# A backward pass of two attention branches: other pieces for the serial chain, another split of the sweep, narrower query blocks, shared transpose tiles

## The chip, the cores and the metric

The kernel runs on one NeuronCore of a Trainium2 chip. A core has five engines with their own instruction queues: TensorE (PE in the profile; PEld is its loading of weights), VectorE (DVE), ScalarE (ACT), GpSimd (POOL) and SyncE (SP), which only issues DMAs here. Each queue runs in order. The metric is the device time of one execution in microseconds, the median of several runs; lower is better.

## The reference

The reference computes an output and the gradients of eleven inputs by jax.vjp. Branch A is attention with 32 query heads of width 18 and one shared key and value head, over 2048 tokens. Branch B is a memory transformer: 64 segments of 32 tokens follow each other, each with 8 memory rows that the segment before has made, 32 heads of width 128. A sigmoid gate mixes the two.

```python
def _B_ref(x, mem0, Wq, Wk, Wv, Wo, seg_len):
    ...
    for s in range(n_seg):
        xs = x[:, s * seg_len:(s + 1) * seg_len, :].copy()
        h = jnp.concatenate([mem, xs], axis=1)
        ...
        o = jnp.einsum('bhte,hed->btd', o, Wo)
        mem = o[:, :M, :].copy()
        outs.append(o[:, M:, :])
    ...
x = A_x
g = _sigmoid((x * gate_w).sum(-1, keepdims=True))
a = _A_ref(x, A_wq, A_wk, A_wv, A_wo)
b = _B_ref(x, B_mem0, B_Wq, B_Wk, B_Wv, B_Wo, B_seg_len)
return g * a + (1 - g) * b
```

What matters: the gradient of branch B runs through the 64 segments backwards, one after the other, as each one's memory gradient is made of the next one's. Branch A has no such order.

## The kernel before

The stages follow each other on all engines: loads and projections (0 to 431 us), the forward chain of branch B woven with pass 1 of branch A (to 2130), `b_bulk` (to 2800), the backward chain of branch B woven with pass 2 of branch A (to 4325), `b_post` (to 4577), `b_dw` (to 5475) and `a_final`. The boundaries are read from the trace.

**Weaving.** TensorE works in order, and a chain would leave it idle while other engines work between its matmuls. So the chain is a Python generator that yields between pieces, and `weave` issues one sweep step of branch A at each yield (`extra` gives more or fewer steps behind single pieces, `lead` some before the first). What is issued is a fixed list per engine; nothing is decided at run time.

**A sweep step** (`a_pass2`) handles 128 queries of a head pair and 512 keys; there are 4 key blocks x 256 = 1024 steps. Two matmuls make the scores b_S (two PSUM banks, one buffer), two make b_dP (single banks, three buffers), ScalarE takes the exponential of b_S into b_E, VectorE multiplies b_dP by b_E in two halves into b_dS, and one step later four matmuls add b_E and b_dS, weighted with the transposed queries and output gradients, into the accumulator b_acc, which stays in one bank over a key block of 256 steps. The queries come from `qs_dram` as tiles b_QS: 512 columns of queries and output gradients, then 512 columns of their transposes, in which each head has 18 columns padded to 32. `a_post`, in pass 1, writes the second half. Before, one load of 256 KB serves four steps, with three buffers. 768 steps (key blocks 0 to 2) go with the backward chain, 256 with `b_dw`.

**The backward chain** (`b_chain_bwd`) has 12 pieces per segment. In order: two projections of the memory gradient with WoT (tiles r_pj and r_x, 20 matmuls each); transposes by matmul (`mem_T`) and the first `mem_grad`; the score gradient pd; 48 units of `heads`, four matmuls each into r_pj, dealt out as 4, 8, 4, 5, 9, 9, 9 with the other two `mem_grad` among them; and the last piece, which makes the next memory gradient dm from hs. r_pj and r_x have one buffer each. Among these sits `kv_mm`, work for later: it forms a 4-head block of token gradients dk or dv for the top 11 token tiles (KVT), 176 blocks, four per segment for the first 12 segments that have them (KV4), then three; `kv_out` moves it out by ScalarE and stores it. The loads of a segment, the DMA transposes of r_dT (`load_dT`, only for the lower 55 segments) and the b_QS loads all go through SP's queue in program order. `extra` adds 8 steps behind three pieces of the first segment, while the weights WT are loaded, and takes one step away in each of segments 4 to 39 (counted in the order in which they run).

**b_bulk** runs 128 groups of four heads through a software pipeline; a tick of the loop runs each stage once, on a group that many ticks back, in the order of the list `order`. The transposes go through PSUM tile x_tr with two buffers: q, k, o, v and dO (four 128x128 blocks each) and, in tiles of their own, one block of P (st_T) and of dS (st_DT). VectorE or ScalarE copies each out and so frees the buffer.

**b_post** takes the token tiles 5 to 0, forms dk and dv (`st_KV`), transposes them (`st_T`) and multiplies with WT (`st_H`). Tile 5 is one of the top 11, whose dk and dv the chain has stored already; `st_KV` forms them again and does not store them.

**b_dw** forms the weight gradients, long runs of matmuls into w_acc, with six sweep steps ahead of them and then one step whenever another WCOLS columns have streamed. Its b_QS loads go through ScalarE's queue.

Matmuls of all parts carry line 84 in the profile, transposes line 89, as helpers issue them; so they are told apart by their tiles.

Of the kernel before, what the change touches and what calls it, by code (L numbers as in the profile page):

```python
# [10 lines left out]
ALU = mybir.AluOpType  # L11
AX = mybir.AxisListType
BF16 = mybir.dt.bfloat16
# [3 lines left out]
P = 128  # L17
# [20 lines left out]
KV4 = 12  # L38
WCOLS = 4800
# [9 lines left out]
class Kern:  # L49
# [606 lines left out]
    def b_bulk(self, wp, lp, sp, psum):  # L656
# [105 lines left out]
        st_QT = lambda t: trans(t, "q", 2)  # L762
        st_KT = lambda t: trans(t, "k", 2)
# [69 lines left out]
        def st_T(t):  # L833
            tt, g, r, d = view(t)
            sc["PT", t] = transp(d["P"], r, "x_PT")

# [39 lines left out]
        def st_DT(t):  # L876
            tt, g, r, d = view(t)
            sc["DT", t] = transp(d["dS"], r, "x_DT")

# [12 lines left out]
        def st_K(t):  # L892
# [12 lines left out]
            if t % 4 == 3:  # L905
                c2 = t // 4 % 2
                for i in range(4):
# [4 lines left out]
        order = [(0, st_QT), (7, B_(0)), (0, st_KT), (7, B_(1)), (5, st_OT), (7, B_(2)), (5, st_VT), (7, B_(3)),  # L912
                 (0, st_GT), (4, st_Om), (9, st_Qm), (3, st_T), (None, st_SDm), (8, st_DT), (2, st_R), (7, st_K),
# [69 lines left out]
    def b_chain_bwd(self, wot, sp, kd, kvp, keep, psum):  # L983
# [119 lines left out]
        for s in reversed(range(NSEG)):  # L1103
# [59 lines left out]
            kv_mm(n0, "r_pj")  # L1163
            kv_out(n0)
# [13 lines left out]
            heads(4)  # L1178
            kv_mm(n0 + 1)
# [4 lines left out]
            kv_out(n0 + 1)  # L1184
# [6 lines left out]
            load_dT(s - 1, 2)  # L1191
# [3 lines left out]
            heads(5)  # L1195
# [4 lines left out]
            heads(9)  # L1200
# [14 lines left out]
            heads(9)  # L1215
# [6 lines left out]
            if s:  # L1222
                PqB = blocks(Pq, "r_PqB")
# [26 lines left out]
    def b_post(self, sp, rp, psum):  # L1250
# [8 lines left out]
        def load_s(n):  # L1259
            tt = NTT - 1 - n  # L1260
            if tt >= 0:
# [9 lines left out]
        def load(c, names):  # L1271
# [3 lines left out]
            d = C.setdefault(c, {})  # L1275
            for w in names:
                if w == "pd":
# [10 lines left out]
        def st_KV(t):  # L1288
            tt, g, r, d = NTT - 1 - t // 8, t % 8, slice(4 * (t % 2), 4 * (t % 2) + 4), C[t // 2]
            pks = []  # L1290
# [9 lines left out]
            for w, pk in zip(("dk", "dv"), pks):  # L1300
# [3 lines left out]
                if t % 2 == 1 and tt < self.NTT - KVT:  # L1304
# [353 lines left out]
    def load_A_kv(self, keep):  # L1658
# [9 lines left out]
        def load(b):  # L1668
            if b < NPR * (self.T // 512):
                p, qb = b // 4, b % 4  # L1670
                self.QD[b] = keep.tile([P, 512], BF16, name="a_QD", bufs=3)
                nc.sync.dma_start(self.QD[b][:], self.qs_dram[p, qb][:, 0, :])
# [23 lines left out]
    def a_qd_end(self, p, qb, pq, absq, sp):  # L1696
# [4 lines left out]
        (nc.sync if qb % 2 == 0 else nc.gpsimd).dma_start(self.qs_dram[p, qb][:, 0, :], QD[:, :])  # L1701
# [69 lines left out]
    def dl_rows(self, t4, sp, psum):  # L1771
# [5 lines left out]
        for i in range(2):  # L1777
            r0 = 32 * (2 + i) + DA
            self.nc.gpsimd.dma_start(self.qs_dram[:, t4, r0:r0 + 2, 0, :], dlT[32 * i:32 * i + 32, :])

    def a_post(self, p, qb, acs, sp, psum, dl_all):
# [16 lines left out]
        tq_.dma_start_transpose(qt[:].rearrange("p a b c -> p a (b c)"), self.qs_dram[p, qb][:, 0, :])  # L1798
# [26 lines left out]
        nc.gpsimd.tensor_tensor(out=qt[:], in0=qt[:],  # L1825
                                in1=rl[:].rearrange("p a b c -> p a (b c)").unsqueeze(3).to_broadcast([P, 4, 4, 32]),
                                op=ALU.mult)
        dq_.dma_start(self.qs_dram[p, qb][:, 1, :], qt[:].rearrange("p a b c -> p (a b c)"))

    def a_pass2(self, keep, sp, psum, kb0, kb1, rd, dkp, nd):  # L1830
        nc = self.nc
        T, NTT = self.T, self.NTT
        KV = {}

        def load_KV(kb):
            if kb < kb1:
# [336 lines left out]
```

## Time and profile before

| | us |
|---|---|
| median of 3 runs (5570.62 to 5579.26) | 5571.51 |
| the profiled execution, its own time | 5579.62 |
| its span | 5577.9 |
| b_bulk, 2130 to 2800 | 670 |
| backward chain with 12 leading steps, 2800 to 4325 | 1525 |
| of it the first segment, 2826 to 2894.6 | 68.6 |
| b_post, 4325 to 4577 | 252 |
| b_dw, 4577 to 5475 | 898 |
| busy over the span: PE, DVE, ACT, POOL | 94%, 64%, 59%, 39% |

The profiled execution is one run, 8 us above the median. In the timeline a line gives the start, the time that the merged instructions took, the engine, the source line, the operation with output and inputs, shapes, the count, and in brackets the idle time of the engine before it and what ended it. Matmuls overlap, so what a group costs is read from start to start and not from its own duration. A busy TensorE is not a TensorE at full rate: short waits do not show as idle time, since the ends of matmuls are modelled. "issue" as the end of an idle time means that the engine waited for nothing that the profile shows.

### The profile page before, as it was taken

To read this page: it belongs to the slowest core of one execution; us is meant where nothing else is said; L and a number is where in the kernel's file an instruction comes from. 1 tells how busy PE (TensorE), PEld (TensorE's weight loads), DVE (VectorE), ACT (ScalarE), POOL (GpSimd) and SP (SyncE) were. 2 spreads that over 40 slices of the span, in tenths; PEclk is the share of its full clock that TensorE was granted. 3 is DMA by queue.
4 is the path that set the end of the run, shared out by engine and by line. 5 is a ranking of instruction groups with operands and counts; after the bars stand their busy time and mean duration, and the time that the engine had idled before them with its cause. 6 is when DMAs were issued, how large, how long until landed. Compare 5 with 4: busy or idle time off the path is not lost. (4 is left out here: it accounts for less than half of the span.)

```text
span 5577.9 us, 221916 instructions
## 1 busy us (share of the span) xinstructions
PE 5256.1 (94%) x96013; PEld 2840.4 (51%) x96013; DVE 3575.6 (64%) x7082; ACT 3308.6 (59%) x4754; POOL 2184.3 (39%) x4185
## 2 busy tenths in 40 slices
PE   8999999999999998899979999999999889999998
PEld 6434444444444445666635555555555666544344
DVE  5337888788888886566567666677777115555441
ACT  4327788788878885555557666667777224434321
POOL 4004555455555544333325555555554111111113
PEclk9999999999999999999979999999999999999999
DMA  6645666666665546888766999999887878565643
GB/s 214 224 170 128 140 137 136 131 137 138 141 136 122 117 101 198 248 247 244 214 228 174 195 190 186 192 193 203 189 190 153 205 186 243 175 192 182 174 138 109
DMA packets 1050281, 978.44 MB, mean 175 GB/s; under 512 B 599027, under 2 KB 865532, under 8 KB 1039699
## 3 DMA queue, kind: packets, MB, share of 16 engines
q1 hardware_dynamic: 934514, 695.47, 53.3%
q0 software_dynamic: 100736, 247.10, 14.3%
q10 hardware_dynamic: 14048, 21.68, 1.2%
q8 instruction: 750, 12.29, 1.0%
q14 instruction: 233, 1.90, 0.1%
HBM read 537.94 MB, written 374.74 MB: 164 GB/s over the span
## 5 line engine op out<-in xcount | busy, mean ns | idle before, releaser
L1890 DVE TENSOR_TENSOR b_dS<-b_dP,b_E 128x512 bf16<-128x512 f32 x2048 | 1312.2, 684 | 722.4 <-PE b_dP L84 343.1
L1750 DVE TENSOR_TENSOR a_W<-a_dP,a_E 128x512 bf16<-128x512 f32 x2048 | 1314.9, 684 | 274.0 <-issue 126.8
L1867 ACT ACTIVATE b_E<-b_S 128x1024 bf16<-128x1024 f32 x1024 | 1048.8, 1024 | 717.6 <-PE b_dP L84 498.5
L1720 ACT ACTIVATE a_E<-a_S 128x1024 bf16<-128x1024 f32 x1024 | 1050.0, 1025 | 257.5 <-PE a_dP L84 170.1
L84 PEld LDWEIGHTS <-b_QS 32*128 32x128 bf16 (+1 forms) x8192 | 232.0, 92 | 585.8 <-issue 546.0
L84 PE MATMUL w_acc<-w_d,w_h 128*128 128x512 bf16 (+1 forms) x2400 | 505.3, 381 | 0.0
L84 PE MATMUL r_pj<-WT,r_dT 128*32 128x288 bf16 x12288 | 474.7, 293 | 7.0 <-issue 4.2
L84 PE MATMUL b_S<-b_KV,b_QS 32*128 32x512 bf16 x2048 | 412.6, 397 | 70.9 <-ACT b_E L1867 47.9
L84 PE MATMUL a_S<-a_QD,l_KV 32*128 32x512 bf16 x2048 | 400.6, 385 | 42.5 <-ACT a_E L1720 35.2
L84 PE MATMUL b_acc<-b_dS,b_QS 128*32 128x512 bf16 x2048 | 435.4, 403 | 1.1 <-DVE b_dS L1890 1.0
L84 PE MATMUL b_acc<-b_E,b_QS 128*32 128x512 bf16 x2048 | 417.6, 404 | 2.3 <-issue 2.3
L84 PE MATMUL a_acc<-a_W,l_WK 128*32 128x512 bf16 x4096 | 414.7, 390 | 4.6 <-issue 4.2
L84 PE MATMUL b_dP<-b_KV,b_QS 32*128 32x512 bf16 x2048 | 415.6, 398 | 2.5 <-DVE b_dS L1890 2.4
L84 PE MATMUL a_acc<-a_E,l_VK 128*32 128x512 bf16 x4096 | 406.2, 382 | 9.4 <-issue 4.6
L84 PE MATMUL a_dP<-a_QD,l_KV 32*128 32x512 bf16 x2048 | 399.7, 386 | 0.0
L84 PEld LDWEIGHTS <-r_dT 128*32 128x32 bf16 x12288 | 331.6, 99 | 103.0 <-issue 28.2
L84 PEld LDWEIGHTS <-w_h 128*128 128x128 bf16 (+1 forms) x2688 | 216.8, 100 | 258.6 <-issue 46.7
L84 PEld LDWEIGHTS <-hm 128*32 128x32 bf16 x7680 | 204.7, 97 | 195.8 <-issue 2.6
L856 POOL TENSOR_TENSOR x_prod<-x_dOT,x_oT 128x512 bf16<-128x512 bf16 x128 | 148.0, 1156 | 269.2 <-ACT x_oT L853 255.3
L84 PEld LDWEIGHTS <-l_KV 32*128 32x128 bf16 x4096 | 122.1, 91 | 253.8 <-issue 209.4
L1431 POOL DMA_DIRECT2D out_dram<-w_o x96 | 52.0, 542 | 452.6 <-DVE w_o L79 240.3
L84 PEld LDWEIGHTS <-l_WK 128*32 128x32 bf16 x4096 | 106.8, 93 | 224.3 <-issue 223.9
(460 smaller groups left out, 10363.0 us busy)
## 6 DMA issues: line engine op xcount, KB each, us to landing
b_QS<-qs_dram SPq DMA_DIRECT2D x192, 256.0 KB
dOx_dram<-p_tok SPq DMA_DIRECT2D x16, 1024.0 KB
c_vx<-vx_dram SPq DMA_DIRECT2D x64, 256.0 KB
krow_dram<-c_k POOLq DMA_DIRECT2D x64, 256.0 KB
qrow_dram<-c_q POOLq DMA_DIRECT2D x64, 256.0 KB
vrow_dram<-c_v POOLq DMA_DIRECT2D x64, 256.0 KB
x_q<-qx_dram SPq DMA_DIRECT2D x32, 512.0 KB
x_dO<-dOx_dram SPq DMA_DIRECT2D x32, 512.0 KB
```

Of the source, the lines that this page charges most:

```text
L84: return self.nc.tensor.matmul(out, lhsT, rhs, start=start, stop=stop, tile_position=tp, skip_group_check=True)
L856: nc.gpsimd.tensor_tensor(out=sc["prod", t][:], in0=sc["dOT", t][:], in1=oT[:], op=ALU.mult)
L1431: nc.gpsimd.dma_start(od[kt * P:kt * P + P, cs], o16[:])
L1720: nc.scalar.activation(E_[n][:], S.pop(n)[:], ACT.Exp, scale=SCALEA)
L1750: nc.vector.tensor_tensor(out=W_[n][:, i, :], in0=dP[i][:], in1=E_[n][:, i, :], op=ALU.mult)
L1867: nc.scalar.activation(E_[n][:], S.pop(n)[:], ACT.Exp, scale=SCALEA)
L1890: nc.vector.tensor_tensor(out=D_[n][:, i, :], in0=dP[i][:], in1=E_[n][:, i, :], op=ALU.mult)
```

## The change

- The chain gets 14 pieces per segment: heads are dealt out as 2, 8, 4, 4, 3, 8, 8, 6, 5, the kv_mm stand in other pieces, all in r_x, with `kv_out` a piece later, and four per segment only for the first 9 (KV4).
- The sweep is split after step 928 and not after 768: 928 steps with the chain (12 leading, 14 a segment, 22 more in the first), 96 in `b_dw`, a step there each 13312 columns. As 928 lies within a key block, the accumulator is stored as part_dram and added again at the end of the block.
- b_QS drops the padding: 18 columns per head in the second half, and one load (2 x 800 columns, 410 KB) serves eight steps, with two buffers. The accumulating matmuls write 18 of 32 partitions of each head, so four matmuls with zeros open each accumulation.
- `b_post` loads dk and dv of tile 5 and forms them no more.
- In `b_bulk` the single transposes of P and dS become a fifth block of the tiles of k and q, earlier in the list; st_T and st_DT are gone, st_Om and st_SDm stand elsewhere.

The diff, cut (left out: the other uses of the new layout, the removal of st_T and st_DT, changed loop bounds):

```diff
 KVT = 11
-KV4 = 12
-WCOLS = 4800
+KV4 = 9
+SWEEP = 928
+QSW = 800
+WCOLS = 13312
 RIDE = 24
...
             due.append([])
-        def transp(d, r, nm):
-            pt = psum.tile([P, 5, P], BF16, name="x_tr", bufs=2)
-            self.tr(pt[:, 0, :], d[:, 1, r, :].rearrange("p i t -> p (i t)"), P)
+        def transp(d, r, nm, pt):
+            self.tr(pt[:, 4, :], d[:, 1, r, :].rearrange("p i t -> p (i t)"), P)
             o = sp.tile([P, 256], BF16, name=nm, bufs=2)
             nc.vector.transpose(o[:, 0:128], d[:, 0, r, :].rearrange("p i t -> p (i t)"))
-            nc.vector.tensor_copy(o[:, 128:256], pt[:, 0, :])
             return o
...
         sc = {}
-        def trans(t, w, nb):
+        def trans(t, w, nb, ride=None):
+            pt = psum.tile([P, 5, P], BF16, name="x_tr", bufs=2)
+            if 0 <= t < NG:
+                tt, g, r, d = view(t)
+                for i in range(4):
+                    self.tr(pt[:, i, :], d[w][:, 4 * (g % 4) + i, :], P)
+            o2 = ride and ride(pt)
+            if 0 <= t < NG:
+                trans_out(t, w, nb, pt)
+            if o2:
+                nc.vector.tensor_copy(o2[:, 128:256], pt[:, 4, :])
+        def trans_out(t, w, nb, pt):
             tt, g, r, d = view(t)
-            pt = psum.tile([P, 5, P], BF16, name="x_tr", bufs=2)
-            for i in range(4):
-                self.tr(pt[:, i, :], d[w][:, 4 * (g % 4) + i, :], P)
             if w == "v":
...
             sc[w + "T", t] = o
-        st_QT = lambda t: trans(t, "q", 2)
-        st_KT = lambda t: trans(t, "k", 2)
+        def ride(t, nm, out):
+            def put(pt):
+                if 0 <= t < NG:
+                    tt, g, r, d = view(t)
+                    sc[out, t] = transp(d[nm], r, "x_" + out, pt)
+                    return sc[out, t]
+            return put
+        st_QT = lambda t: trans(t, "q", 2, ride(t - 8, "dS", "DT"))
+        st_KT = lambda t: trans(t, "k", 2, ride(t - 3, "P", "PT"))
         st_GT = lambda t: trans(t, "dO", 7)
...
         B_ = lambda i: lambda t: st_B(t, i)
-        order = [(0, st_QT), (7, B_(0)), (0, st_KT), (7, B_(1)), (5, st_OT), (7, B_(2)), (5, st_VT), (7, B_(3)),
-                 (0, st_GT), (4, st_Om), (9, st_Qm), (3, st_T), (None, st_SDm), (8, st_DT), (2, st_R), (7, st_K),
+        order = [(None, st_QT), (7, B_(0)), (None, st_KT), (7, B_(1)), (4, st_Om), (5, st_OT), (7, B_(2)), (5, st_VT),
+                 (7, B_(3)), (None, st_SDm), (0, st_GT), (9, st_Qm), (2, st_R), (7, st_K),
                  (None, st_SDx), (1, st_M), (4, st_Ox), (9, st_Qx)]
...
             self.expand(dSB[:], dS[:].rearrange("p a (u q) -> p (a u) q", q=8), 16)
-            kv_mm(n0, "r_pj")
-            kv_out(n0)
             yield
...
                                 start=(wi == 2 and u + cp == 0), stop=(wi == 1 and u + cp == 8), tp=(0, 32 * g))
-            heads(4)
-            kv_mm(n0 + 1)
+            heads(2)
+            kv_mm(n0)
             pad_in("ds", dS[:, 1, :])
...
             yield
-            kv_out(n0 + 1)
+            kv_out(n0)
             heads(8)
...
             heads(4)
+            mem_cols(0, mem_grad("r_x", ((rows(L["kx"]), blk(dSB)), (rows(mrow["k"]), blk(dSB, 8)))))
+            yield
+            mem_cols(1, mem_grad("r_x", ((rows(mrow["dx"]), [perm] * 8), (rows(mrow["q"]), blk(dSqB)))))
+            heads(4)
             load_dT(s - 1, 2)
-            mem_cols(0, mem_grad("r_x", ((rows(L["kx"]), blk(dSB)), (rows(mrow["k"]), blk(dSB, 8)))))
-            yield
-            mem_cols(1, mem_grad("r_x", ((rows(mrow["dx"]), [perm] * 8), (rows(mrow["q"]), blk(dSqB)))))
-            heads(5)
             if s:
...
             yield
-            heads(9)
+            heads(3)
+            kv_mm(n0 + 1)
+            yield
+            kv_out(n0 + 1)
+            heads(8)
             if s:
...
             yield
-            heads(9)
+            heads(8)
             load_dT(s - 1, 0)
-            if n1 - n0 == 4:
-                kv_mm(n0 + 2)
-                kv_out(n0 + 2)
             if s:
...
             yield
-            heads(9)
+            heads(6)
+            if n1 - n0 == 4:
+                kv_mm(n0 + 2)
+            if s:
+                PqB = blocks(Pq, "r_PqB")
+            yield
+            if n1 - n0 == 4:
+                kv_out(n0 + 2)
+            heads(5)
             hp = sp.tile([64, 2 * GD], F32, name="r_hp", tag="r_dSB", bufs=1)
...
                 kv_load(1)
-            if s:
-                PqB = blocks(Pq, "r_PqB")
             yield
...
             d = C.setdefault(c, {})
+            if tt >= self.NTT - KVT:
+                names = [{"q": "dk", "dO": "dv"}.get(w, w) for w in names if w != "pd"]
             for w in names:
+                if w in ("dk", "dv"):
+                    d[w] = rp.tile([P, 8, P], BF16, name=f"y_l{w}", bufs=3)
+                    nc.sync.dma_start(d[w][:].rearrange("p h e -> p (h e)"),
+                                      self.xtok[w][tt * P:(tt + 1) * P, h0 * P:h0 * P + 1024])
+                    continue
                 if w == "pd":
...
             tt, g, r, d = NTT - 1 - t // 8, t % 8, slice(4 * (t % 2), 4 * (t % 2) + 4), C[t // 2]
+            if tt >= self.NTT - KVT:
+                return
             pks = []
...
         T = self.T
-        self.qs_dram = dram.tile([NPR, 4, P, 2, 512], BF16, name="qs_dram")
+        self.qs_dram = dram.tile([NPR, 2, P, 2, QSW], BF16, name="qs_dram")
+        self.part_dram = dram.tile([P, 512], F32, name="part_dram")
         self.kv_dram = dram.tile([P, T], BF16, name="kv_dram")
...
         dq_.dma_start(otd(self.dqtok_dram), dq[:].rearrange("p a b c -> p a (b c)"))
-        nc.gpsimd.tensor_tensor(out=qt[:], in0=qt[:],
-                                in1=rl[:].rearrange("p a b c -> p a (b c)").unsqueeze(3).to_broadcast([P, 4, 4, 32]),
+        qc = sp.tile([P, 4, 4, DA], BF16, name="a_qc", bufs=1)
+        nc.gpsimd.tensor_tensor(out=qc[:], in0=qt[:, :, :, 0:DA],
+                                in1=rl[:].rearrange("p a b c -> p a (b c)").unsqueeze(3).to_broadcast([P, 4, 4, DA]),
                                 op=ALU.mult)
-        dq_.dma_start(self.qs_dram[p, qb][:, 1, :], qt[:].rearrange("p a b c -> p (a b c)"))
-    def a_pass2(self, keep, sp, psum, kb0, kb1, rd, dkp, nd):
+        dq_.dma_start(self.qs_dram[p, qb // 2][:, qb % 2, 512:QSW], qc[:].rearrange("p a b c -> p (a b c)"))
+    def qs_q(self, p, qb):
+        return self.qs_dram[p, qb // 2][:, qb % 2, 0:512]
+    def a_pass2(self, keep, sp, psum, lo, hi, rd, dkp, nd):
         nc = self.nc
-        T, NTT = self.T, self.NTT
+        NS = NPR * self.NTT
...
         def load(c):
-            if c < NC:
-                p, q4 = (c // 4) % NPR, c % 4
-                QS = sp.tile([P, 2, 512], BF16, name="b_QS", bufs=3)
-                rd.dma_start(QS[:], self.qs_dram[p, q4])
-                Q[c] = (QS[:, 0, :], QS[:, 1, :].rearrange("p (a b) -> p a b", b=P))
-        def pair(n):
-            return kb0 + n // (NPR * NTT), n // 4, n % 4
+            if 8 * c < hi:
+                Q[c] = sp.tile([P, 2, QSW], BF16, name="b_QS", bufs=2)
+                rd.dma_start(Q[c][:], self.qs_dram[(c // 2) % NPR, c % 2])
...
-        load(0)
-        load(1)
...
+        load(lo // 8)
+        part = None
+        if lo % NS:
+            part = sp.tile([P, 512], F32, name="b_prt", bufs=1)
+            rd.dma_start(part[:], self.part_dram[:, :])
...
-                if n % 4 == 2:
-                    load(n // 4 + 2)
+                if n % 8 == 1:
+                    load(n // 8 + 1)
...
                 o = n - 1
-                if o % NS == 0:
+                if o == lo or o % NS == 0:
                     acc = psum.tile([P, 512], F32, name="b_acc", bufs=1)
-                SD = Q[o // 4][1]
+                    for k in range(4):
+                        self.mm(acc[:, k * P:k * P + P], lhsT=self.zeros[:], rhs=self.zeros[:], start=True, stop=False)
+                last = o % NS == NS - 1
                 src = (D_.pop(o), E_.pop(o))
                 for i4 in range(4):
-                    self.mm(acc[32 * i4:32 * i4 + 32, :], lhsT=SD[:, o % 4, 32 * i4:32 * i4 + 32],
-                            rhs=src[i4 // 2][:, i4 % 2, :],
-                            start=(o % NS == 0), stop=(o % NS == NS - 1), tp=(0, 32 * i4))
-                if o % NS == NS - 1:
+                    w = 512 + 4 * DA * (o % 4) + DA * i4
+                    self.mm(acc[32 * i4:32 * i4 + DA, :], lhsT=Q[o // 8][:, o // 4 % 2, w:w + DA],
+                            rhs=src[i4 // 2][:, i4 % 2, :], start=False, stop=last or o == hi - 1, tp=(0, 32 * i4))
+                if last:
                     dkv = dkp.tile([P, 4, P], BF16, name="r_kvo", bufs=2)
...
+                    if part is None:
+                        nc.scalar.copy(flat, acc[:])
+                    else:
+                        nc.vector.tensor_tensor(out=flat, in0=acc[:], in1=part[:], op=ALU.add)
+                        part = None
...
+                elif o == hi - 1:
+                    pt = sp.tile([P, 512], F32, name="b_pto", tag="b_E", bufs=3)
+                    nc.scalar.copy(pt[:], acc[:])
+                    nc.gpsimd.dma_start(self.part_dram[:, :], pt[:])
             yield
...
                     SB("rk") as rk, SB("rv") as rv, SB("rd") as rd, PS("rp") as rp, PS("a3p") as a3p:
-                extra = {4: 8, 6: 8, 7: 8}
-                extra.update({12 * q: -1 for q in range(4, 40)})
-                k.weave(k.b_chain_bwd(rw, rs, rd, rv, rk, rp), k.a_pass2(a3k, a3s, a3p, 0, 3, nc.sync, rv, 3), 12,
-                        extra, k.load_WT, 12)
+                k.weave(k.b_chain_bwd(rw, rs, rd, rv, rk, rp), k.a_pass2(a3k, a3s, a3p, 0, SWEEP, nc.sync, rv, 3), 12,
+                        {4: 8, 7: 6, 9: 8}, k.load_WT, 12)
             wHs = ExitStack()
...
             with SB("a4s") as a4s, PS("a4p") as a4p, PS("wp") as wp_:
-                k.b_dw(ws, wA, wB, wH, wp_, k.a_pass2(a4s, a4s, a4p, 3, 4, nc.scalar, a4s, 2))
+                k.b_dw(ws, wA, wB, wH, wp_, k.a_pass2(a4s, a4s, a4p, SWEEP, 4 * NPR * k.NTT, nc.scalar, a4s, 2))
             with SB("a5s") as a5s, PS("a5p") as a5p:
```

More of the change, by code (lines that the diff above doesn't have):

```diff
@@ L1303, in st_KV @@
                 nc.scalar.copy(d[w][:, r, :], pk[:])
-                if t % 2 == 1 and tt < self.NTT - KVT:
+                if t % 2 == 1:
                     h0 = 8 * (t // 2 % 4)
@@ L1867, in ex @@
             nc.scalar.activation(E_[n][:], S.pop(n)[:], ACT.Exp, scale=SCALEA)
[L1869 to L1879 removed]
+        load(lo // 8)
[3 more added lines that the diff above has]
+            rd.dma_start(part[:], self.part_dram[:, :])
+        mm_S(lo)
+        ex(lo)
+        acc = None
+        for n in range(lo, hi + 1):
+            if n < hi:
+                if n % 8 == 1:
+                    load(n // 8 + 1)
                 if n % NS == NS // 2:
[L1881 to L1882 removed]
+                    load_KV(n // NS + 1)
+                if n + 1 < hi:
                     mm_S(n + 1)
@@ L1885, in a_pass2 @@
                 mm_u([t[:] for t in dP], n, 64)
-                if n + 1 < NP_:
+                if n + 1 < hi:
                     ex(n + 1)
```

42 lines of the change are left out of this document (13 added, 29 removed).

## The prediction

> **What bounds the kernel now.** I read the slices first, then the windows by stage, the waits of TensorE in the stages the change touches, and single pieces in the timeline.
>
> ```profile
> PE   8999999999999998899979999999999889999998
> DVE  5337888788888886566567666677777115555441
> DMA  6645666666665546888766999999887878565643
> ```
>
> ```profile
> core 0: us, PE busy (x) PEld busy (x) DVE busy (x) ACT busy (x) POOL busy (x), PEclk, DMA share, GB/s
> 2130.00:2800.00 670.00, 590.04 (x14886) 449.78 (x14882) 394.78 (x1439) 351.22 (x724) 247.60 (x298) 0.97 0.80 238
> 2894.60:4325.00 1430.40, 1365.11 (x32408) 767.62 (x32407) 1018.17 (x1819) 995.69 (x1402) 754.25 (x1374) 0.97 0.85 184
> 4325.00:4577.00 252.00, 231.84 (x3500) 181.48 (x3500) 42.04 (x117) 56.05 (x103) 31.90 (x57) 0.94 0.78 187
> 4577.00:5475.00 898.00, 875.45 (x6276) 409.88 (x6277) 441.45 (x747) 326.89 (x367) 151.12 (x249) 0.98 0.63 187
> ```
>
> The slices show TensorE at 9 nearly throughout, VectorE at 5 to 8. In the windows the rows are b_bulk, b_chain_bwd without its first segment, b_post and b_dw. TensorE is over 95% busy in the second and fourth. A sweep step moved from the fourth to the second therefore saves its TensorE time there and costs it here; the question is the two prices.
>
> **Price of a step in b_dw.** The timeline of a steady stretch:
>
> ```profile
> 5001.50 0.39 PE L84 MATMUL b_S<-b_KV,b_QS 32*128 32x512 bf16 x2
> ...
> 5001.83 0.39 PE L84 MATMUL b_acc<-b_dS,b_QS 128*32 128x512 bf16 x2
> 5002.16 2.12 PE L84 MATMUL w_acc<-w_d,w_h 128*128 128x512 bf16 x9
> ```
>
> From the step's start to the next w_acc is 0.66 us, and the pipeline is refilled behind it: 13 steps from 5001.50 to 5037.76 take 36.26 us, of which 121.9 matmuls (4800 columns of 512 each) at 0.2165 us (nine start to end 2.12, eight 1.90) are 26.4, so a step costs 0.75. 256 - 96 = 160 steps go: **-119 us**. At 5180 the chain that ended last waits 21.86 us for one b_QS load, and TensorE idles 5.5 us of it and restarts at half clock; with a step every 13312 columns instead of 4800 a load has more than twice the time: -8. The first 150 us of the stage have a DMA share of 0.75 to 0.93, and with fewer steps the big w_d loads have less time there: I add 4 (0 to 10). Together **-123**.
>
> **Price of a step in the chain.** A piece is what stands between two b_S. Its period, read from start to start:
>
> ```profile
> 2900.97 0.39 PE L84 MATMUL b_S<-b_KV,b_QS 32*128 32x512 bf16 x2
> 2901.52 0.66 PE L84 MATMUL r_pj<-WT,r_dT 128*32 128x288 bf16 x16
> 2902.52 0.39 PE L84 MATMUL b_S<-b_KV,b_QS 32*128 32x512 bf16 x2 [0.34 <-ACT b_E L1867]
> ...
> 4009.17 0.39 PE L84 MATMUL b_S<-b_KV,b_QS 32*128 32x512 bf16 x2
> 4009.72 1.28 PE L84 MATMUL r_pj<-WT,r_dT 128*32 128x288 bf16 x36
> 4010.93 0.39 PE L84 MATMUL b_S<-b_KV,b_QS 32*128 32x512 bf16 x2
> ```
>
> Nine units of heads (36 matmuls): 1.76. Eight: 1.64. So n units take 0.66 + 0.122 n. Four should take 1.15 and take 1.55, with TensorE idle until the exponential of ScalarE releases the one b_S buffer: 1.55 is a floor under every piece. A kv_mm (4 + 16 matmuls) adds 0.66. The other pieces are kept: first projection 2.05, second 1.74, mem_T and first mem_grad 1.68, pd alone 1.55, heads(4) with mem_grad 1.64, mem_grad with heads(5) 1.88, last piece 1.67.
>
> The new segment with three kv, piece by piece: 2.05, 1.74, 1.68, pd 1.55, heads(2)+kv 1.58, heads(8) 1.64, heads(4)+mem_grad 1.64, mem_grad+heads(4) 1.76, heads(3)+kv 1.69, heads(8) 1.64, heads(8) 1.64, heads(6) 1.55, heads(5) 1.55, last 1.67: sum 23.38. Three pieces lie on the floor. A fourth kv lifts heads(6) to 2.05: 23.88. Without kv: 23.21. Now the same segments take, undisturbed, 21.8 (three kv, twelve steps), 21.17 (three kv, eleven steps, by `extra`), 21.82 (four kv, eleven) and 20.7 (none).
>
> 63 segments after the first, now: 8 x 20.7 + 12 x 21.82 + 24 x 21.17 + 19 x 21.8 = 1350 us. They take 1430. With KV4 = 9, after: 7 x 23.21 + 9 x 23.88 + 47 x 23.38 = 1476. So **+126** undisturbed, 0.79 a step: by itself the move loses a little.
>
> The 80 us between 1350 and 1430 are gaps of another kind:
>
> ```profile
> 3520.90 0.29 PE L84 MATMUL r_pj<-r_kr,r_ks 32*32 32x128 bf16 x8 [1.07 <-issue]
> 3521.47 0.61 PE L84 MATMUL b_acc<-b_dS,b_QS 128*32 128x512 bf16 x2
> ```
>
> and in the waits of TensorE from 2895 to 4325:
>
> ```profile
> PE r_x L84 <- issue: 14.4, 13, 2.1
> PE r_pj L84 <- issue: 12.2, 15, 1.4
> ```
>
> In the first, TensorE stops in the middle of kv_mm with nothing to wait for, and afterwards a matmul takes 0.61 instead of 0.39 for some 3 us: half clock. In the packets of q8 (instruction, 16 KB each) one starts 0.2 to 2 us ahead of nearly every such gap, so I read them as late instruction blocks, late because the DMA engines are full. Segments without the dT transposes (2957 to 3043, DMA share 0.65) and without kv (4221 to 4304, 0.75) have none; 3850 to 4199 has 0.88 and loses 1.44 us a segment; 3044 to 3742 has 0.91 and loses 1.93. DMA work per segment is 0.875 x 349 / 15 = 20.3 us. The compact blocks make a step's b_QS 51.2 KB instead of 64, so 14 steps carry 717 KB where 12 carried 768: about 20.1. Over 23.38 us that is a share of 0.86 undisturbed, where the two stretches have 0.93 and 0.99. Between 0 at 0.75 and 1.44 at 0.93 I take 0.85 us, for 52 segments with transposes and kv: 44 instead of 80. Chain stage: +126 - 36 = **+90**. Ends: 0 (gaps vanish) and 93 (they grow with the 16% more steps).
>
> The Trainium skill, Runtime: NRT & Kernel Launch, section Instruction fetch mechanics, says that instructions are fetched in blocks of 16 KiB by a DMA queue of the sequencer's own, and that the cost of crossing a block is mostly hidden. By that rule the gaps are not late blocks, and fewer DMA bytes take none away; the trace speaks against it (the 1.07 us above), but the rule is a rival below.
>
> **Other parts.** The compact weights have 18 columns for 32; no row has 18, a 128x32 load takes 97 ns and a 128x8 one 86, and both lie beside matmuls of 0.39 us: 0, the nearest row being the 128x32 one; 11 ns on all 4096 loads, exposed, would be 45 us in either direction. The four zero matmuls per accumulator and the part_dram store and load are under 3 us in all. The smaller POOL multiply in a_post is in a stage where POOL is half idle: 0. First loads of 410 KB instead of 256: +1. The first segment keeps its 36 steps.
>
> b_post: tile 5 no longer forms dk and dv. One kv pair costs TensorE 1.3 us of a 4.6 us tick, 8 ticks: -10. At the start
>
> ```profile
> PE y_pk L84 <- DMA y_mR<-qrow_dram: 14.3, 1, 14.3
> ```
>
> is the last of 15 loads issued one after the other on SP's queue (0.4 to 0.7 each); dk and dv of one chunk are two. -10 if the transposed dq doesn't end later, 0 if it does; I take -5: **-15** (-5 to -22).
>
> b_bulk: in a clean tick (4.385 us, 4.685 with st_K) TensorE waits for the x_tr buffer of st_QT, which VectorE frees late:
>
> ```profile
> 2754.09 0.41 PE L84 MATMUL x_b<-WoN,x_oT 128*128 128x288 bf16 x2
> 2754.62 0.38 PE L89 MATMUL x_tr<-identB,x_o 128*128 128x128 bf16 x4
> ```
>
> 0.28 us over the 0.25 of two x_b. The loop is: st_GT's transposes, +0.42 to VectorE, its chain of 2.84 through the qT copy to OT's start, then OT to GT 1.12: 4.38. After: the four small operations move behind M, into the loop between M and the kT copy: 0.42 + 3.1 + 0.8 = 4.32, and 4.56 with st_K, as VT now waits for KT's buffer. -0.1 x 128 = **-12**; if TensorE sets the pace instead (3.9) -60, if the buffers held longer cost more, +15.
>
> **Sum.** -123 + 90 - 15 - 12 + 1 = -59. The profiled execution took 5579.6 (span 5577.9), the runs' median is 5571.5; I take the difference over: **5512**.
>
> **Rivals.**
> - Gaps stay (80 us, or 93): nothing in the DMA share helps. 5548 to 5561. For: 3742 to 3850 has a share of 0.96 and no gap, so the share is not all. This is also what the skill's rule would give. 0.22.
> - Gaps vanish: 5468. For: 4221 to 4304. 0.18.
> - Slower: VectorE's queue. Its pair of b_dS takes 1.25 of a period, and dS, two 32x32 transposes and hs add 0.28 to 0.45 in the very pieces that shrink to 1.55. If b_acc then waits 0.3 us in four pieces, a segment takes 1.2 more: 63 x 1.2 = 76, 5588. It decides from 1.15 us a segment. Against: 1.55 - 1.25 leaves 0.3, and the pd piece without kv keeps 1.55 today. 0.10.
> - The small parts bring nothing (b_bulk, b_post 0): 5539. 0.10, inside the range.
> - My forecast: 0.40, own range 5490 to 5535.
>
> The range 5450 to 5585 takes in the first two rivals, the bounds of b_bulk and most of the third. Within 0.2% (5560 to 5583), about what a measurement here can tell from no change: 0.08, from the first and fourth together. Slower 0.10. Faster 0.82.
>
> **What would show it.** The chain stage (first projection to the last dm transposes) should last 1498 + 90, b_dw 775, b_post 237, b_bulk 655. Undisturbed segments of 23.4 with 14 b_S pairs show the prices right; 24.5 with idle before b_acc shows the third rival. "issue" in the chain's waits of TensorE should fall from 31 us to about 17. The forecast is wrong if a b_QS load becomes late (two buffers of eight steps, issued six steps ahead), or if b_dw waits for w_d.

## The result, and the profile after

The changed kernel takes 5537.1 us (median of 6 runs, 5530.8 to 5552.2), the kernel before in the same comparison 5571.1 (5556.4 to 5589.7): a ratio of 0.9942, 95% interval 0.9918 to 0.9965. In a later comparison it gave 0.9933 (0.9908 to 0.9958). The forecast was 5512 with a range of 5450 to 5585: the time lies inside it, 25 us above the forecast and 2 us above the narrower range of 5490 to 5535. The medians differ by 34 us, the two profiled executions by 48.8, as the one before lay 8 us above its median and this one 6 below. The profiled execution took 5530.8 us, its span is 5529.1.

First the slices of the page after (the span in 40 parts, busy tenths), then the windows by stage: b_bulk, the chain without its first segment, b_post, b_dw.

```profile
PE   8999999999999998999979999999999988999998
DVE  5337888888888887656668777777777812333322
DMA  6646766766665546888765788787877687856653
```

```profile
core 0: us, PE busy (x) PEld busy (x) DVE busy (x) ACT busy (x) POOL busy (x), PEclk, DMA share, GB/s
2130.00:2777.00 647.00, 584.43 (x14868) 423.95 (x14868) 389.67 (x1434) 358.84 (x721) 245.06 (x291) 0.97 0.82 245
2870.60:4425.80 1555.20, 1456.57 (x33703) 786.25 (x33701) 1224.89 (x2139) 1156.62 (x1564) 756.30 (x1374) 0.98 0.76 169
4425.80:4657.80 232.00, 218.23 (x3179) 171.60 (x3177) 41.49 (x115) 46.13 (x85) 32.27 (x58) 0.96 0.72 197
4657.80:5428.40 770.60, 754.20 (x5029) 392.75 (x5030) 239.70 (x429) 166.31 (x207) 151.54 (x249) 0.98 0.67 203
```

In the slices VectorE now stays at 7 to 8 until the chain's end and falls to 1 to 3 behind it: the sweep steps have moved. In the second window TensorE is busy for 1456.6 of 1555.2 us; 98.6 us are idle where 65.3 were. Stage by stage, cut at the first projection of the chain, at the last transposes of dm, at the last y_pdx and at the last w_acc (seen in the trace):

| stretch, us | before | after | difference | forecast |
|---|---|---|---|---|
| up to the chain's first projection | 2826.1 | 2802.7 | -23.4 | -12 (b_bulk) |
| backward chain | 1498.7 | 1623.1 | +124.4 | +90 |
| b_post | 251.4 | 232.0 | -19.4 | -15 |
| b_dw | 903.5 | 770.6 | -132.9 | -123 |
| rest | 98.2 | 100.7 | +2.5 | +1 (loads) |
| span | 5577.9 | 5529.1 | -48.8 | -59 |

One term stands out: the chain is 34 us above its forecast. The waits of TensorE in the chain's 63 later segments (what it waited for, us in total, times, longest):

```profile
PE b_S L86 <- ACT b_E L1888: 32.4, 140, 0.6
PE b_S L86 <- DMA b_QS<-qs_dram: 21.6, 13, 4.2
PE r_x L86 <- issue: 9.4, 11, 2.1
PE r_pj L86 <- issue: 6.7, 9, 1.4
PE r_x L86 <- DMA r_kr<-qx_dram: 6.0, 3, 2.5
PE b_acc L86 <- issue: 2.4, 2, 1.7
PE b_S L86 <- issue: 1.7, 3, 0.8
```

The second line is new: there was no wait for b_QS in the chain before. The stops that end in issue sum to 20.2 us, where before they were 31.2 (17 were expected). So the stops that I had argued about shrank nearly as forecast, and another kind of wait took their place. One of its places, first in SP's queue (start, time, operation), then SP's longest wait in total over the chain, then the whole core in three stretches, then TensorE:

```profile
3553.52 1.28 SPq L1035 DMA_TRANSPOSE r_dT<-dvx_dram  x1
3554.86 0.63 SPq L1023 DMA_DIRECT2D r_kx<-kx_dram  x1
3555.55 0.48 SPq L1025 DMA_DIRECT2D r_k<-krow_dram  x1
3556.07 1.35 SPq L1874 DMA_DIRECT2D b_QS<-qs_dram  x1
3557.47 0.43 SPq L1069 DMA_DIRECT2D r_kvS<-pq_dram  x1
```

```profile
SPq L1035 <- PE r_pj L86: 248.6, 67, 7.3
```

```profile
3551.00:3555.00 4.00, 4.00 (x100) 2.26 (x93) 3.21 (x6) 3.25 (x5) 3.23 (x6) 1.00 0.12 40
3555.00:3563.50 8.50, 7.98 (x191) 4.54 (x190) 7.36 (x13) 6.26 (x9) 2.31 (x6) 1.00 1.07 194
3563.50:3567.50 4.00, 0.02 (x4) 0.03 (x4) 0.21 (x1) 0.05 (x1) 0.00 (x0) 0.82 0.43 121
```

```profile
3563.11 0.19 PE L86 MATMUL r_pj<-selz,r_hx 128*32 128x16 bf16 x4
3567.48 0.61 PE L86 MATMUL b_S<-b_KV,b_QS 32*128 32x512 bf16 x2 [4.18 <-DMA b_QS<-qs_dram]
...
3570.69 0.60 PE L86 MATMUL b_S<-b_KV,b_QS 32*128 32x512 bf16 x2
```

The load of b_QS is issued behind a DMA transpose of r_dT and the loads r_kx and r_k, and in front of those of r_kvS and r_kvR. The column before the last of the windows is the DMA share: 0.12 before this burst, 1.07 in it (packets that start in a window count with their whole time, hence above 1). The load is issued at 3556.07 and TensorE is let go at 3567.48, 11.4 us later; at two other places it is 10.6 (3358.23 to 3368.85) and 10.1 (3457.86 to 3467.91).

Six steps at 23.08 / 14 = 1.65 us are 9.9, but the load does not get them. SP's queue works in order, and the transpose in front of the load waits until the matmuls into r_pj have read the old r_dT (4.5 us here, 248.6 in the chain). So the load is issued 2.4 us after TensorE has passed the step at which the program places it. TensorE was ready for it 4.18 us before 3567.48, at 3563.30: only 7.2 us after the issue, and 7.2 and 7.3 at the two other places.

TensorE stands still for 4.2 us and then works at half clock for some 5 us (a matmul takes 0.61 for 0.39; the granted clock from 3567.5 to 3573 is 0.51); the next segment takes 25.2 us instead of 23.1. As 14 steps a segment and 8 a load meet every fourth segment (56 steps, 7 loads), a load falls into this burst in every fourth segment. Eleven of the 13 late loads stand right behind r_dT, r_kx and r_k; they take 7.7 to 11.4 us from the issue until TensorE goes on.

### The profile page after: what moved, and what is told of

It is laid out like the page before. It is cut to its first block, busy times and chain, and to the rows that moved or that the text cites. A ratio compares the mean times of both kernels' runs of the same rounds, so it can differ in the third digit from the quotient of the medians.

```text
span 5529.1 us, 221015 instructions
## 1 busy us (share of the span) xinstructions
PE 5202.2 (94%) x95713; PEld 2806.3 (51%) x95713; DVE 3576.1 (65%) x7083; ACT 3308.1 (60%) x4738; POOL 2163.1 (39%) x4186
## 5 line engine op out<-in xcount | busy, mean ns | idle before, releaser
L1888 ACT ACTIVATE b_E<-b_S 128x1024 bf16<-128x1024 f32 x1024 | 1048.7, 1024 | 629.3 <-PE b_dP L86 546.3
L86 PE MATMUL r_pj<-WT,r_dT 128*32 128x288 bf16 x12288 | 489.9, 290 | 5.2 <-issue 5.2
L86 PE MATMUL w_acc<-w_d,w_h 128*128 128x512 bf16 (+1 forms) x2400 | 484.6, 380 | 0.0
L86 PE MATMUL b_acc<-b_dS,b_QS 128*18 128x512 bf16 x2048 | 422.5, 396 | 2.2 <-issue 1.7
L86 PE MATMUL b_acc<-b_E,b_QS 128*18 128x512 bf16 x2048 | 409.4, 396 | 0.6 <-issue 0.6
L86 PE MATMUL x_b<-WoN,x_oT 128*128 128x288 bf16 x1024 | 211.3, 290 | 3.5 <-issue 3.5
```

The lines of the kernel that those rows point to most:

```text
L86: return self.nc.tensor.matmul(out, lhsT, rhs, start=start, stop=stop, tile_position=tp, skip_group_check=True)
L1888: nc.scalar.activation(E_[n][:], S.pop(n)[:], ACT.Exp, scale=SCALEA)
```

## Experiments

Each is compared with the kernel before on the chip it ran on. "Chain" is the whole chain stage of the profiled execution; the waits are those of TensorE in the 63 later segments, and "issue stops" are its stops that end in issue. All in us.

| kernel | ratio (95% interval) | chain | wait for b_QS | issue stops | wait for r_kr |
|---|---|---|---|---|---|
| before | 1 | 1498.7 | 0 | 31.2 | 0.6 |
| after | 0.9942 (0.9918 to 0.9965) | 1623.1 | 21.6 | 20.2 | 6.0 |
| after again | 0.9933 (0.9908 to 0.9958) | 1628.4 | 20.4 | 23.7 | 6.2 |
| four-step loads, four buffers | 0.9849 (0.9826 to 0.9873) | 1578.4 | 0 | 14.0 | 5.8 |
| the same, three buffers | 0.9863 (0.9838 to 0.9888) | 1599.2 | 17.0 | 13.5 | 7.0 |
| padded blocks | 1.0007 (0.9988 to 1.0027) | 1640.6 | 61.5 | 9.1 | 2.0 |
| four buffers, split 768 | 0.9898 (0.9874 to 0.9922) | 1477.5 | 0 | 20.2 | 10.1 |
| four buffers, 12 pieces, split 768 | 0.9887 (0.9862 to 0.9911) | 1483.1 | 0 | 22.3 | 2.4 |
| four buffers, no r_dT transposes | one execution | 1540.5 | 0 | 0.8 | 2.1 |
| four buffers, kv loads earlier | 0.9807 (0.9781 to 0.9833) | 1561.2 | 0 | 12.4 | 0 |
| four buffers, heads even | 0.9832 (0.9803 to 0.986) | 1572.5 | 0 | 15.3 | 7.4 |
| both of these | 0.9811 (0.9786 to 0.9836) | 1554.5 | 0 | 11.2 | 0 |
| after, old b_bulk | 0.9926 (0.9902 to 0.995) | 1625.5 | 23.0 | 23.0 | 5.8 |
| both of these, old b_bulk | 0.9833 (0.9804 to 0.9862) | 1566.8 | 0 | 19.3 | 0 |

The last two rows have the chain of "after" and of "both of these" unchanged. So two executions of one chain can differ by 12 us in the chain and by 8 us in the issue stops, and smaller differences between two rows show nothing.

**The late loads.** The theory: a load that is placed six steps ahead lands too late when it stands in the burst. The rival: the DMA engines are full, so whatever is not late in b_QS is late elsewhere.

```diff
-            if 8 * c < hi:
-                Q[c] = sp.tile([P, 2, QSW], BF16, name="b_QS", bufs=2)
-                rd.dma_start(Q[c][:], self.qs_dram[(c // 2) % NPR, c % 2])
+            if 4 * c < hi:
+                Q[c] = sp.tile([P, QSW], BF16, name="b_QS", bufs=4)
+                rd.dma_start(Q[c][:], self.qs_dram[(c // 4) % NPR, c // 2 % 2][:, c % 2, :])
...
-                if n % 8 == 1:
-                    load(n // 8 + 1)
+                if n % 4 == 1:
+                    load(n // 4 + 3)
```

> The changed kernel with its b_QS blocks loaded four steps at a time (205 KB) into four buffers: the same SBUF and the same bytes, but a load is issued ten steps before its first use instead of six. Theory (late b_QS loads): in the backward chain TensorE waits 21.6 us for b_QS in 13 places and the eight segments behind the larger gaps take about 12 us more at half clock. Both go: chain stage 1623 -> about 1590, total about 5503, waits of b_S for b_QS near 0. Rival (full DMA engines): the same bytes pass in the same bursts, so what is late only changes its name (r_kr, instruction blocks): chain stage 1615 to 1625, total 5530 to 5540.

The waits for b_QS are gone, the chain takes 1578.4 us and the ratio is 0.9849. Nearly nothing else got later (r_vmT once, 0.9 us): in the waits of this kernel

```profile
PE r_pj L86 <- issue: 6.3, 9, 1.3
PE r_x L86 <- DMA r_kr<-qx_dram: 5.8, 4, 2.2
PE r_x L86 <- issue: 4.5, 7, 1.3
```

r_kr stays where it was and issue did not rise (20.2 to 14.0). The rival is refuted: the same bytes fit, they only had to be asked for earlier. The 44.7 us of the chain are the 21.6 of waits and mostly the half clock behind them (196 matmuls of the sweep took over 0.5 us after, 82 here; the granted clock is at 0.5 for 75 us of the 63 segments after, for 31 here). That the late loads are no accident of one profile:

> The changed kernel itself once more, on the chip of this call. Theory: ratio to the kernel before 0.994 as in its first runs (0.992 to 0.9965), so that the runs with four-step loads lie about 0.9% below it; late b_QS loads again about 20 us in a dozen places, as they follow from the order of the program and not from chance. Rival: the late loads are an accident of the one profile, under 8 us here.

They come again, 20.4 us in 13 places; the theory holds. Next, lead or size? Three buffers instead of four, and `load(n // 4 + 2)`: half the load, but the lead of six steps back again.

> The four-step loads of compact blocks with three buffers instead of four: a load is issued six steps ahead of its first use, as in the changed kernel, but is half as large. Theory (the lead decides: a load that is issued in the burst of r_dT, r_kx and r_k takes 10 to 11 us to land, and six steps of 1.65 us are 9.9): the late loads come back, waits of b_S for b_QS 15 to 40 us, chain stage 1600 to 1620. Rival (the size decides: 410 KB take twice the packets of 205 KB): no late loads, chain stage about 1578 as with four buffers.

```profile
PE b_S L86 <- DMA b_QS<-qs_dram: 17.0, 12, 2.5
```

The lead decides whether any load is late: a load of half the size is late in 12 places. The chain gives back 21 of the 45 us. The size counts too. Right behind r_dT, r_kx and r_k the lead, from the issue until TensorE is ready for the block, is 7.2 us in the median in both kernels; 11 of 14 loads are late there in the changed kernel, 9 of 28 here. With four buffers it is at least 13.4 us, and none is late. In the kernel before it was 9.0 to 10.8 at this place, and none was late. No run moved the load alone in front of the transpose. The layout of before, 256 KB for four steps (`QSW = 1024`, 32 columns a head, three buffers, `if n % 4 == 2: load(n // 4 + 2)`), has a lead of five steps:

> The changed kernel with the padded query blocks of before (1024 columns, 32 per head, 256 KB for four steps, three buffers, issued as before two loads ahead); pieces, split, b_bulk and b_post stay changed. Theory: its loads come in time, as before, so the 34 us of late b_QS go; but 14 steps carry 896 KB instead of 717, and the stops of TensorE that end in issue grow from 20 us to about 30: chain stage about 1600, total about 5515. Rival (the layout matters only through the lateness): total equal to the four-step loads of compact blocks, about 5503. Second rival (the DMA engines are the limit): late loads of other tiles appear, total 5540 or more.

```profile
PE b_S L86 <- DMA b_QS<-qs_dram: 61.5, 35, 4.1
```

My theory was wrong here: these loads do not come in time. Five steps lasted 9.1 us before (21.8 / 12 = 1.82 a step) and last 8.2 now, and 35 loads are late; the whole gain of the change is gone (1.0007). So in this kernel the padded blocks with their shorter lead cost 0.65% of the time. That the shorter step alone makes them late is not shown: the new pieces also move the transposes in SP's queue, and half of the late loads have 4.6 us or less between issue and need. That the issue stops rise with the bytes did not show either: they are 9.1. A TensorE that waits elsewhere may let its instructions catch up; no run separates that.

**The stops that end in issue.** Are they late instruction blocks, late because the DMA engines are busy? `load_dT` issues its DMA in one segment only, so this kernel leaves out most of the transposes; the matmuls on r_dT stay, on old contents.

```diff
         def load_dT(s, wi):
-            if 0 <= s < NSEG - KR:
+            if s == NSEG - KR - 1:
```

> The four-step loads (four buffers) with the DMA transposes of r_dT left out in all segments but the first that has them; the matmuls on r_dT stay, on old contents, so the token gradients of branch B are not those of the reference. It takes the largest user of the DMA engines out of the chain. Theory (the stops of TensorE that end in issue are late instruction blocks, late because the DMA engines are busy): the share of the DMA engines in the chain falls from 0.78 to 0.5 or less, the issue stops fall from 14 us to under 4, and no r_kr is late: chain stage about 1535. Rival (crossing a block costs what it costs, whatever else the DMA engines do): issue stops stay at 12 to 16 us.

The window of the 63 segments, and all issue rows of the waits:

```profile
2869.40:4343.70 1474.30, 1423.49 (x33703) 780.46 (x33701) 1223.67 (x2139) 1154.65 (x1564) 758.71 (x1374) 1.00 0.55 149
```

```profile
PE b_acc L86 <- issue: 0.3, 1, 0.3
PE r_x L86 <- issue: 0.3, 1, 0.3
PE r_pj L86 <- issue: 0.2, 1, 0.2
```

The DMA share is 0.55 and the stops are 0.8 us instead of 14.0, with the same matmuls. This is one execution, but the step is larger than the 8 us between executions: the stops come with the transposes. That they are late instruction blocks is not shown by this run; the times speak for it. In 27 of the 32 stops before, and in 15 of the 19 with four-step loads, TensorE goes on 1.2 to 1.6 us after a 16 KB packet of q8 has ended, where such a packet comes every 5.7 us. What makes a block late stays open: the packets themselves last as long with the transposes as without (median 1.10 and 1.08 us). The Trainium skill, Runtime: NRT & Kernel Launch, section Instruction fetch mechanics, says that crossing a block costs little as it is mostly hidden; that agrees with this run and not with the others, where the stops sum to 9 to 31 us over as many blocks. The share alone doesn't order them: 9.1 us at 0.77, 23.0 at 0.75, 22.3 at 0.85.

**The move and the pieces.** Split back to 768/256, with 14 pieces of which two (three in 35 segments) issue no step:

```diff
-SWEEP = 928
+SWEEP = 768
-WCOLS = 13312
+WCOLS = 4800
...
-                        {4: 8, 7: 6, 9: 8}, k.load_WT, 12)
+                        {**{14 * q + j: -1 for q in range(1, 64) for j in ((4, 9, 11) if 4 <= q < 39 else (4, 11))}, 4: 8, 7: 6, 9: 8}, k.load_WT, 12)
```

> The kernel of the run before (four-step loads, four buffers) with the split of the sweep put back to 768/256: the 14 pieces stay, but two of them in a segment (three in 35 segments) issue no step. Theory: a step costs 0.79 us in the chain without late loads and 0.75 in b_dw, so the move by itself is worth almost nothing: total within 10 us of that run, chain stage about 126 shorter, b_dw about 125 longer. Rival (the move is where the gain comes from, since gaps shrink with fewer b_QS loads in b_dw and the steps hide in the chain): this one is 30 us or more slower than the run before.

The windows of chain and b_dw, first with the split at 768, then at 928 (four-step loads in both):

```profile
2898.60:4308.30 1409.70, 1351.30 (x32419) 753.97 (x32417) 1021.97 (x1819) 1002.29 (x1402) 753.43 (x1373) 0.99 0.81 180
...
4538.80:5437.60 898.80, 872.07 (x6237) 412.04 (x6311) 441.60 (x748) 327.80 (x368) 151.56 (x249) 0.98 0.61 183
```

```profile
2885.50:4395.50 1510.00, 1440.97 (x33704) 785.55 (x33702) 1225.61 (x2139) 1156.26 (x1564) 756.45 (x1374) 0.99 0.78 173
...
4629.10:5401.50 772.40, 751.01 (x4972) 392.62 (x5031) 239.94 (x429) 166.49 (x207) 151.53 (x249) 0.98 0.67 202
```

160 steps cost 126.4 us in b_dw, 0.79 each, and 100.9 in the chain stage (1578.4 - 1477.5), 0.63 each. The undisturbed segments say nearly the same: 23.08 with fourteen steps and 21.89 with twelve in the same pieces, 0.60 a step. The move is worth 25 us, and the ratio says the same (0.9849 against 0.9898). My theory that it is worth nothing fell; the rival's 30 us is near. The pieces alone: `b_chain_bwd`, `KV4` and `extra` of before on the same loads.

> Four-step loads of compact blocks, b_bulk and b_post as changed, but the backward chain with the 12 pieces, KV4 = 12 and the split 768/256 of before. Theory (the 14 pieces carry steps and bring nothing else; compact blocks take gaps away): undisturbed segments as before (21.2 with eleven steps), 63 segments in about 1410 instead of 1430, chain stage about 1477 as in the run that has 14 pieces and 768 steps, ratio 0.990. Rival (compact blocks take no gaps away; the 14 pieces did): 63 segments in 1425 to 1440, ratio 0.994. Second rival (14 pieces cost by themselves): chain stage 1460 or less, ratio 0.986.

1483.1 against 1477.5, and 0.9887 against 0.9898: the 14 pieces show no effect by themselves, as expected; they are there so that the steps find a place. The 63 segments take 1414.2 instead of the 1430.2 of the kernel before, so compact blocks in four buffers may take some 16 us of gaps away, if not by the share, which is 0.85 in both. That is little more than two executions of one chain differ by, and rests on one profile of each; it stays open.

**b_bulk.** The function of before in the changed kernel:

> The changed kernel with the b_bulk of before: single transposes of P and dS in x_tr tiles of their own. Theory: in the profile a tick of b_bulk lasts 4.936 us before and 4.772 after on the mean although the undisturbed tick is the same (4.39 and 4.69 before, 4.41 and 4.70 after), so it is the disturbed ticks that got fewer, and that comes with the order: total about 5558, mean tick 4.93. Rival (the disturbed ticks differ from run to run and not by the order): mean tick 4.77 to 4.80, total 5530 to 5540.

> The fastest kernel so far (four-step loads, kv loads one block earlier, heads 2, 7, 4, 4, 3, 7, 7, 7, 7) with the b_bulk of before. Theory (the new order of b_bulk takes disturbance away: mean tick 4.94 and 4.88 in the two profiles with the old order, 4.81 on the mean of ten with the new one): 10 us or 0.2% slower than that kernel, ratio about 0.983, mean tick above 4.85. Rival (the order is worth nothing, the mean tick differs from run to run by more than between the orders): ratio 0.981 or below, mean tick inside 4.76 to 4.94.

The first gave a ratio of 0.9926 (0.9902 to 0.995) and a mean tick of 4.875 us, between theory and rival in the tick and no slower than the changed kernel (0.9942 and 0.9933). The second gave 0.9833 (0.9804 to 0.9862), where the theory put it, but with a mean tick of 4.751, shorter than in all but one of the profiles with the new order, which lie between 4.727 (the three buffers) and 4.935 (the padded blocks). So the theory falls: the mean tick differs by 0.21 us, 26 us in all, among executions of one and the same b_bulk, and the 21 us between the two profiles of the case say nothing on the order. A gain or loss within 0.2% stays open.

**A faster version.** Two more edits on the four-step loads: the loads of the kv work one block earlier (`kv_load(n + 3)`, one more at the start), and the heads dealt out as 2, 7, 4, 4, 3, 7, 7, 7, 7.

> The four-step loads (four buffers) with the loads of the kv work (r_kr, and kvS, kvR, r_ks with it) issued one block earlier, three ahead instead of two, into the same three buffers. Theory (what is left of late loads are four r_kr between 3070 and 3180 us, 5.8 us, and half a clock behind them): these go, chain stage 6 to 9 shorter, total 6 to 9 below. Rival (a load that now waits for the kv matmuls stands in SP's queue and holds up what is behind it): b_QS or the loads of the next segment get late, total 5 or more above.

> The four-step loads (four buffers) with the 48 units of heads dealt out as 2, 7, 4, 4, 3, 7, 7, 7, 7 instead of 2, 8, 4, 4, 3, 8, 8, 6, 5. Theory (every piece lasts at least 1.55 us, set by the one buffer of b_S, and above it 0.66 + 0.122 per unit): three pieces go from 1.64 to 1.55 and two stay at 1.55, so a segment loses 0.27 us, the waits of b_S for b_E fall from 36 to about 20 us, chain stage 17 shorter, total about 17 below the kernel with the old dealing. Rival (the pieces are bound by ScalarE or VectorE over the whole segment, so the idle time moves with the units): no change, within 5 us.

> Four-step loads (four buffers), the kv loads one block earlier and heads dealt out as 2, 7, 4, 4, 3, 7, 7, 7, 7 together. Theory: no b_QS and no r_kr is late, and the undisturbed segment is 23.0 instead of 23.1: chain stage 1550 to 1565, ratio to the kernel before 0.978 to 0.982, 1.2% or more below the changed kernel. Rival (what is gained by earlier loads turns into other stops, as the DMA engines carry the same bytes in less time): stops that end in issue rise above 20 us, chain stage above 1575.

Earlier kv loads take r_kr out of the waits; the 63 segments are 14 us shorter, of which the waits for r_kr were 5.8; the rest, half clock behind them or the difference of two executions, is not separated. In time it is 0.9807 against 0.9849, with intervals that overlap. The even heads bring what the price says in their own pieces (three fall from 1.63 to 1.55) but the segment loses 0.08 us and not 0.27: the heads end later, so the last piece grows from 1.57 to 1.63 and the first projection waits longer for dm. In time that is 0.9832 against 0.9849, no clear gain. Both together, 0.9811 (0.9786 to 0.9836), are no better than the kv loads alone (0.9807) in the timing, though the chain is the shortest of those that do all the work, 1554.5. The fastest versions are 1.9% below the kernel before and some 1.3% below the changed one. Its waits in the chain, from the top:

```profile
PE b_S L86 <- ACT b_E L1889: 19.0, 78, 0.6
PE r_x L86 <- issue: 5.8, 9, 2.4
PE r_pj L86 <- issue: 3.1, 5, 0.9
```

## Why the prediction was right in sign and range, and where it failed

- **b_dw, -123.** Measured -132.9. The step price was put at 0.75 (the 36.26 and 26.4 us shown for it give 0.76), it is 0.79 (126.4 / 160). The waits for b_QS in the stage fell from 9.8 to 4.8 us; w_d is waited for 0.8 us only.
- **Undisturbed segments, +126.** Measured +111: 7 x 22.9 + 9 x 24.05 + 47 x 23.08 = 1461 against 1350. The prices of the pieces hold: in the kernel with four-step loads, at 3590 us, heads(8) takes 1.63, heads(3) with kv_mm 1.68, mem_grad with heads(4) 1.75, heads(6) 1.55, where 1.64, 1.69, 1.76, 1.55 were forecast. The last piece and the first projection were put too high: 1.57 + 1.94 where 1.67 + 2.05 stood.
- **Gaps 80 to 44: the step that failed.** They are 1555.2 - 1461 = 94 us. The reason is not the one of the rival that gives 93: the stops that end in issue fell from 31.2 to 20.2, near the 17 of the forecast, though they differ by 8 between executions. But "a b_QS load becomes late (two buffers of eight steps, issued six steps ahead)" had been named as what would make the forecast wrong, and no time had been put against it. Six steps are 9.9 us by the program; behind the transpose 7.2 are left, and the load takes 7.7 to 11.4 there. With four-step loads the gaps are 1510.0 - 1461 = 49, where 44 had been forecast. The late loads are the missing 45 us. The way to the 44, by the share of the DMA engines, is not borne out either: the stops do not follow the share (22.3 us at 0.85, 23.0 at 0.75); without the transposes they are gone.
- **"By itself the move loses a little"** compared 0.79 with 0.75. The 0.79 compares two chains that differ in more than their steps; step by step it is 0.63. The row was there: the segments with eleven and twelve steps, 21.17 and 21.8, differ by 0.63.
- **b_post, -15.** Measured -19.4; its first ticks last 3.39 and not 4.6 us, and the first y_pdx comes 16 us after the chain instead of 25.
- **b_bulk, -12.** The profile says -21, but the undisturbed ticks are the same, 4.41 and 4.70 for 4.385 and 4.685. The working was wrong, and what the order is worth can't be seen.
- **VectorE's queue,** the rival on the slow side: b_acc waits for b_dS 0.2 us in all. It did not come.

The sum came out right to 10 us in the profile by luck, because an error of +50 in the gaps met errors of -15 in the undisturbed segments, -10 in b_dw, -11 ahead of the chain and -4 in b_post. In the medians, 34 us instead of 59, it is right in sign and range only.

## What to carry to other kernels

When a block gets larger and its buffers fewer, put the lead of the load in us (steps ahead times the new, shorter step, less what the queue holds it back) beside the time from issue to landing in the busiest place of its queue, not beside the mean DMA share. The same SBUF cut into smaller blocks gives a longer lead: 2 x 8 steps gave six steps, 4 x 4 give ten, for 45 us. And read the price of moved work from rows that differ in that work only.

## What the runs showed of the hardware

- A load on SP's queue was late for two reasons: it was issued late behind a transpose that waits (2.4 us after its place in the program), and it landed late in the burst. The Trainium skill, DMA: Bandwidth & Descriptors, section Queues, rings and completion order, says that SP's DMAs share one ring on each of the 16 DMA engines and are taken up in ring order; the trace fits that, though no run gave the load another queue: behind the transposes, r_kx and r_k, a load of 410 KB took 7.7 to 11.4 us until TensorE went on, in a core whose DMA share over the stage is 0.76.
- Stops of TensorE for instructions, as I read those that end in issue, depend on the other DMA traffic: 0.8 us without the transposes at a share of 0.55, 9 to 31 us with them at 0.75 to 0.85, in one and the same stage.
- A wait costs more than itself: behind 4.18 us of idle time TensorE ran at half clock for some 5 us. Over the 63 segments the late loads cost 21.6 us of waiting and, at half clock, about as much again (75 us at a granted clock of 0.5 against 31 without them).
